# Second half of the first row tile's tokens moved from SyncE's DMA queue to ScalarE's, behind that engine's first operation

## Chip, cores and metric

The kernel runs on one core of a Trainium2 chip. The metric is device time in microseconds for one execution. Before the change the median of three runs is 414.63 us (414.38 to 415.16).

## What is computed

One block with two branches over 2048 tokens of width 448, mixed by a gate per token. Branch A is an attention with 16 heads of 28, in which each token looks at 8 keys, its own and those 2, 4, ... 14 tokens back; branch B is a two-layer network of width 1792 with a squared ReLU.

```
x = A_x                                        # (1, 2048, 448)
g = sigmoid((x * gate_w).sum(-1, keepdims=True))
q, k, v = split(x @ wqkv)                      # 16 heads of 28
a = softmax(q . k[pos - 0, 2, ..., 14] * 28**-0.5) @ v, then @ wo
b = relu(x @ w1 + b1)**2 @ w2 + b2
out = g * a + (1 - g) * b
```

The host hands x over transposed (`xT`), as four row tiles of 512 tokens; each tile has the 448 features as three full groups of 128 partitions and a fourth group of 64 that is stored twice, one copy in each half of the partitions. `wqkv`, `w1` and `wo` are laid out in the same four groups.

## The kernel before, in words

Every matrix product is made of three TensorE products: both operands are split into a rounded part ("high") and a remainder ("low"), and high times high, high times low and low times high are added up in PSUM. A split of an operand is a copy to the rounded type on ScalarE (for one half tile a copy on VectorE) and a subtraction on VectorE.

The kernel has an order written out by hand: the instructions of each engine stand in the order in which the program names them, and a small list of due times decides where loads, splits and attention pieces are put between matmuls. TensorE first makes q, k and v for the four row tiles, writes them to DRAM by way of ScalarE and SyncE's queue, and then makes the two layers of branch B and the output projection, while GpSimd and VectorE work through the attention from copies in SBUF.

All loads and stores of the kernel before are issued by SyncE (SP), one after the other, in program order. The loop at L633 to L640 issues the first ones: for each feature group `k` the q weights (`raws[0]`, called `wqraw` in the profile, L635 and L638), then the first row tile's features (`rx`, called `xraw`, L640). For group 0 the row tile comes in two transfers, tokens 0 to 255 and tokens 256 to 511, for the other groups in one. Ten transfers come out of this loop: weights 0, first token half 0, second token half 0, weights 1, tokens 1, weights 2, tokens 2, two halves of weights 3, tokens 3. Behind them SP issues the k and v weights (L645, L648). Completion counts are kept in eight semaphores that the transfers take in turn; a transfer that is the next user of a semaphore waits at the queue until the one before it has landed.

The splits of the first tile stand at L650 to L663: for each group the weights' high part on ScalarE (L651), the two token halves' high parts (ScalarE L658; group 0's first half on VectorE, L656), then the low parts on VectorE (L659 weights, L661 tokens). TensorE's first products are those of `qkv_first`: group 0 of the q products for 128-token blocks 0 and 1 (six matmuls), then for blocks 2 and 3 (six matmuls, which read the second token half), then groups 1 and 2 in the same way (all L258), then group 3 and the k and v products (L187). Ahead of them TensorE runs 13 matmuls on zeros (L628). `none` is a single element that VectorE sets to zero at L626.

Of the kernel before, what the change touches and what calls it, by code (L numbers as in the profile page):

```python
# [9 lines left out]
AF = mybir.ActivationFunctionType  # L10
# [12 lines left out]
CH = 512  # L23
# [33 lines left out]
def gated_mix_kernel(ctx: ExitStack, tc: tile.TileContext, xT, wqkv, w1, w2, wo, b1, b2, out):  # L57
    nc = tc.nc
# [42 lines left out]
    b1t, none = b1z[:, :NF], b1z[0:1, 15:16]  # L101
# [393 lines left out]
    def raw_tile(name):  # L495
        return rawp.tile([P, 4, 512], F32, tag="raw", name=name)
# [135 lines left out]
    rx = raw_tile("xraw0")  # L632
    for k in range(4):  # L633
        if k < 3:
            nc.sync.dma_start(raws[0][:, k, :NQ], wqkv[0, :, k])  # L635
        else:
            for b, rows in ((0, slice(0, 64)), (1, slice(64, P))):
                nc.sync.dma_start(raws[0][rows, k, :NQ], wqkv[b, rows, k])  # L638
        for cols in ((slice(0, 256), slice(256, CH)) if k == 0 else (slice(0, CH),)):
            nc.sync.dma_start(rx[:, k, cols], xT[0, :, k, cols])  # L640

    for b, tag in ((1, "k"), (2, "v")):
        raw = attp.tile([P, 3, D], F32, tag=tag, name=f"wqraw{b}")
# [525 lines left out]
```

## Time and profile before

| | |
|---|---|
| median of three runs | 414.63 us |
| the profiled execution | 414.51 us |
| its span, first to last instruction | 412.7 us |
| TensorE busy | 408.2 us, 99% |
| GpSimd, VectorE, ScalarE busy | 268.5, 255.7, 211.3 us |
| mean granted TensorE clock | 1.000 |

Times in the views count from the first instruction. A row of the timeline gives the start, the duration, the engine, the line and the operation with output and input, a count where neighbours were merged, and in brackets how long the engine stood idle before it and what released it. PEld is the weight load of TensorE, SPq the queue of SyncE in which DMA instructions are issued. The duration of an SPq row is that of the issue, not of the transfer; when a transfer has landed is seen from the instruction that waited for it.

### The profile page before, as it was taken

To read this page: it belongs to the slowest core of one execution; us is meant where nothing else is said; L and a number is where in the kernel's file an instruction comes from. 1 tells how busy PE (TensorE), PEld (TensorE's weight loads), DVE (VectorE), ACT (ScalarE), POOL (GpSimd) and SP (SyncE) were. 2 spreads that over 40 slices of the span, in tenths; PEclk is the share of its full clock that TensorE was granted. 3 is DMA by queue.
4 is the path that set the end of the run, shared out by engine and by line. 5 is a ranking of instruction groups with operands and counts; after the bars stand their busy time and mean duration, and the time that the engine had idled before them with its cause. 6 is when DMAs were issued, how large, how long until landed. Compare 5 with 4: busy or idle time off the path is not lost.

```text
span 412.7 us, 9327 instructions
## 1 busy us (share of the span) xinstructions
PE 408.2 (99%) x3835; PEld 378.0 (92%) x3835; DVE 255.7 (62%) x404; ACT 211.3 (51%) x477; POOL 268.5 (65%) x167
## 2 busy tenths in 40 slices
PE   8999999999999999999999999999999999999997
PEld 7999999999999999888888888989898888888996
DVE  4520433276767766777656798879576677891354
ACT  4641656388765565444565535444653254346540
POOL 0000001955999999989989899999899977940000
DMA  7989999969362315555112649764146630168304
GB/s 226 380 324 326 268 393 299 335 213 311 101 235 104 128 42 218 209 184 152 29 58 95 228 160 270 197 146 149 27 163 186 229 129 2 45 177 132 96 0 180
DMA packets 65611, 73.76 MB, mean 179 GB/s; under 512 B 32352, under 2 KB 58528, under 8 KB 65184
## 3 DMA queue, kind: packets, MB, share of 16 engines
q1 hardware_dynamic: 65568, 73.16, 55.1%
q8 instruction: 30, 0.49, 0.5%
q14 instruction: 13, 0.11, 0.1%
HBM read 45.71 MB, written 28.25 MB: 179 GB/s over the span
## 4 chain that ended last, share of the span: by engine, by line
PE 97%; DMA 1%; SPq 0%; DVE 0%; ACT 0%; issue 0%
PE b L187 33%; PE h L187 32%; PE qkv L187 23%; PE a L187 7%; PE qkv L258 1%; DMA xraw<-xT 1%; PE a L943 1%; PE last L943 0%; SPq L640 0%; SPq L635 0%; DVE bt L822 0%; ACT x L658 0%; PE last L935 0%; PE a L935 0%
## 5 line engine op out<-in xcount | busy, mean ns | idle before, releaser
L334 POOL TENSOR_TENSOR qk<-q,k 128x896 f32<-128x896 f32 x64 | 135.1, 2137 | 84.8 <-DMA k<-k_d 76.4
L341 POOL TENSOR_TENSOR av<-lg,v 128x896 f32<-128x896 f32 x64 | 119.4, 1961 | 6.3 <-DVE lg L335 5.8
L187 PE MATMUL qkv<-wqh,x 64*128 64x448 f32 (+1 forms) x528 | 89.1, 361 | 0.0
L615 DVE TENSOR_TENSOR h<-h,h 128x512 fp32r<-128x512 f32 x56 | 38.4, 688 | 65.9 <-ACT h L618 65.5
L187 PEld LDWEIGHTS qkv<-wqh,x 64*128 64x128 f32 x528 | 72.2, 184 | 0.8
L187 PE MATMUL qkv<-wql,x 64*128 64x448 f32 (+1 forms) x264 | 72.2, 360 | 0.0
L187 PE MATMUL b<-w2ah,h 64*128 64x448 f32 x448 | 68.5, 359 | 0.0
L187 PE MATMUL b<-w2bh,h 64*128 64x448 f32 x448 | 67.8, 360 | 0.0
L335 DVE TENSOR_REDUCE lg<-qk 128x32 f32<-128x896 f32 x64 | 67.0, 1074 | 0.0
L349 DVE TENSOR_REDUCE o<-av 128x112 f32<-128x896 f32 x64 | 66.4, 1070 | 0.1
L616 ACT ACTIVATE h<-h,b1z 128x512 f32<-128x512 f32 x56 | 36.7, 655 | 43.6 <-PE h L187 43.6
L187 PEld LDWEIGHTS b<-w2ah,h 64*128 64x128 f32 x448 | 46.9, 184 | 2.8
L187 PEld LDWEIGHTS b<-w2bh,h 64*128 64x128 f32 x448 | 45.3, 184 | 3.2 <-ACT h L567 0.3
L187 PEld LDWEIGHTS qkv<-wql,x 64*128 64x128 f32 x264 | 44.5, 184 | 0.4
L187 PE MATMUL b<-w2al,h 64*128 64x448 f32 x224 | 44.3, 358 | 0.0
L187 PE MATMUL b<-w2bl,h 64*128 64x448 f32 x224 | 43.2, 358 | 0.0
L206 ACT ACTIVATE st<-qkv 128x448 f32<-128x448 f32 x48 | 24.3, 546 | 34.8 <-PE qkv L187 26.9
L617 ACT ACTIVATE h<-h 128x512 fp32r<-128x512 f32 x56 | 33.5, 598 | 1.7
L618 ACT ACTIVATE h<-h 128x512 f32<-128x512 f32 x56 | 33.3, 594 | 0.0
L187 PE MATMUL h<-x,w1h 64*128 64x512 f32 x168 | 32.8, 386 | 0.0
L567 ACT ACTIVATE h<-h 128x4 fp32r<-128x4 f32 (+1 forms) x35 | 7.2, 207 | 43.1 <-PE b L187 43.0
L187 PE MATMUL h<-x2b,w1h 64*128 64x512 f32 x168 | 28.2, 386 | 0.0
(145 smaller groups left out, 728.7 us busy)
## 6 DMA issues: line engine op xcount, KB each, us to landing
k<-k_d SPq DMA_DIRECT2D x8, 840.0 KB, 6.4
v<-v_d SPq DMA_DIRECT2D x8, 840.0 KB, 4.8
x_d<-x SPq DMA_DIRECT2D x11, 512.0 KB, 6.6
q_d<-st SPq DMA_DIRECT2D x8, 448.0 KB, 4.1
k_d<-st SPq DMA_DIRECT2D x8, 448.0 KB, 4.6
v_d<-st SPq DMA_DIRECT2D x8, 448.0 KB, 5.9
w1raw<-w SPq DMA_DIRECT2D x4, 896.0 KB, 9.2
q<-q_d SPq DMA_DIRECT2D x8, 448.0 KB, 3.6
```

The costliest lines, as they stand in the source:

```text
L187: nc.tensor.matmul(acc.pt[:, :acc.n], a[rows], w[rows], start=acc.todo == acc.all, stop=acc.todo == 1)
L206: nc.scalar.activation(st[:, :, t % 2], pt[:, :D].rearrange("p (g c) -> p g c", g=G), AF.Copy)
L258: nc.tensor.matmul(acc.pt[:, :NQ], a, w, start=k == j == 0, stop=False)
L334: nc.gpsimd.tensor_mul(pr, q[:, s:s + 1].to_broadcast([P, W, C]), k[:, s:s + W])
L335: pending.append(lambda: nc.vector.tensor_reduce(lg[:, s], pr.rearrange("p w (h d) -> p w h d", h=HG), axis=AX.X, op=ALU.add))
L341: nc.gpsimd.tensor_mul(pr.rearrange("p (h d) w -> p w h d", h=HG), lg[:, s][:, :, :, None].to_broadcast([P, W, HG, DH]), v[:, s:s + W].rea ...
L349: nc.vector.tensor_reduce(o[:, g * C:(g + 1) * C], pr, axis=AX.X, op=ALU.add)
L567: nc.scalar.activation(ap, f32(ap), AF.Copy)
L615: nc.vector.tensor_sub(hl, pt, f32(hh))
L616: ops += [lambda pt=pt, r=r: nc.scalar.activation(pt, pt, AF.Relu, bias=b1t[:, f + r:f + r + 1]), lambda pt=pt, hh=hh: nc.scalar.activatio ...
L617: lambda pt=pt, hh=hh: nc.scalar.activation(hh, pt, AF.Square),
L618: lambda pt=pt, r=r, low=low: (nc.scalar.activation(pt, pt, AF.Square), at(delays[r], low))]
```

## The change

The second half of the tokens of group 0 is no longer issued by SP between the first half and the weights of group 1. ScalarE issues it, on its own queue. Just before it, a new copy of one element (`none`) into the first element of the region that the transfer will write is put at the head of ScalarE's stream; since the transfer overwrites that element, it waits for the copy. Bytes, destination and readers of the transfer stay as they were. On ScalarE the load of the function table now stands ahead of the new copy instead of ahead of the first weight copy, then come the new copy, the issue of the transfer, and the splits as before. On SP the nine other transfers of the loop follow in the same order, with nothing in the place of the moved one. The order of TensorE, VectorE and GpSimd is unchanged. As the semaphores are taken in turn, the k and v weight loads of L645 behind the loop wait for other transfers than before: the first for weights 1 (before: second token half 0), the second for tokens 1 (before: weights 1), the third for second token half 0 (before: tokens 1).

```
-        for cols in ((slice(0, 256), slice(256, CH)) if k == 0 else (slice(0, CH),)):
-            nc.sync.dma_start(rx[:, k, cols], xT[0, :, k, cols])
+        if k == 0:
+            nc.sync.dma_start(rx[:, k, :256], xT[0, :, k, :256])
+
+            nc.scalar.activation(rx[0:1, k, 256:257], none, AF.Copy)
+            nc.scalar.dma_start(rx[:, k, 256:], xT[0, :, k, 256:])
+        else:
+            nc.sync.dma_start(rx[:, k], xT[0, :, k])
```

## Prediction

> **What bounds the kernel now.** I read the page first, then what TensorE waits for, then the chain of waits over the first 16 us, then the timeline there, and last the DMA engines' share by microsecond.
>
> ```profile
> span 412.7 us, 9327 instructions
> PE 408.2 (99%) x3835; PEld 378.0 (92%) x3835; DVE 255.7 (62%) x404; ACT 211.3 (51%) x477; POOL 268.5 (65%) x167
> PE 97%; DMA 1%; SPq 0%; DVE 0%; ACT 0%; issue 0%
> ...
> PE warm L628 <- DVE b1z L626: 1.2, 1, 1.2
> PE qkv L258 <- ACT x L658: 0.3, 1, 0.3
> ...
> 7.69:409.68 401.99, 401.99 (x3810) 372.72 (x3810) 252.60 (x396) 208.00 (x472) 267.70 (x154) 1.00 0.56 179
> ...
> 2.13 0.43 SPq L635
> 2.56 0.04 issue
> 2.60 4.59 DMA xraw<-xT
> 7.20 0.02 issue
> 7.22 0.42 ACT x L658
> 7.64 0.04 issue
> 7.69 5.09 PE qkv L258 x24
> 12.78 3.28 PE qkv L187 x27
> ```
>
> TensorE has only two waits in the whole run: 1.2 us ahead of its matmuls on zeros, and 0.3 us ahead of the matmul at 7.69. From 7.69 to its last matmul, which ends at 409.68, it is busy for 401.99 of 401.99 us. So the time is the moment of that matmul plus a fixed rest: 414.51 - 7.69 = 406.82 us. The matmul at 7.69 is the first of feature group 1, and the chain says what it waits for: tokens 1, issued at 2.60 as SP's fifth transfer, land at 7.20, ScalarE copies their first half until 7.64. Whatever the change does, it does it by moving this moment, or by making a new wait behind it.
>
> ```profile
> 0.74 1.28 ACT L651 ACT_TABLE_LOAD   x1 [0.74 <-PEq L1161]
> 0.75 0.39 SPq L635 DMA_DIRECT2D wqraw<-wqkv  x1
> 1.20 0.89 SPq L640 DMA_DIRECT2D xraw<-xT  x2
> ...
> 3.45 0.58 ACT L651 ACTIVATE wqh<-wqraw 128x450 fp32r<-128x450 f32 x1 [1.42 <-DMA wqraw<-wqkv]
> 4.17 1.09 PE L258 MATMUL qkv<-wqh,x 128*128 128x450 f32 x2
> 5.27 0.58 SPq L640 DMA_DIRECT2D xraw<-xT  x1
> 5.42 0.42 ACT L658 ACTIVATE x<-xraw 128x256 fp32r<-128x256 f32 x1 [1.39 <-DMA xraw<-xT]
> 5.89 0.30 PEld L258 LDWEIGHTS qkv<-wqh,x 128*128 128x128 f32 x2 [0.17 <-ACT x L658]
> 6.05 0.58 ACT L651 ACTIVATE wqh<-wqraw 128x450 fp32r<-128x450 f32 x1 [0.21 <-DMA wqraw<-wqkv]
> 6.41 0.56 PE L258 MATMUL qkv<-wql,x 128*128 128x450 f32 x2
> 6.81 0.56 PE L258 MATMUL qkv<-wqh,x 128*128 128x450 f32 x2
> 9.22 0.72 ACT L658 ACTIVATE x<-xraw 128x256 fp32r<-128x256 f32 x2 [0.76 <-DMA xraw<-xT]
> 9.82 0.96 PE L258 MATMUL qkv<-wqh,x 128*128 128x450 f32 x4
> ```
>
> The moved transfer is the second of the pair at 1.20; its reader is ScalarE's copy at 5.42, and the six matmuls that need it begin with the weight load at 5.89. They come in pairs 0.40 apart (6.41, 6.81), so the six are through and the slot for group 1 is free at 7.21. Two numbers follow. First, group 1 cannot start before 7.21 without the moved half landing earlier, so there are 7.69 - 7.21 = 0.48 us to be won. Second, from the half's landing to the free slot it is 7.21 - 5.42 = 1.79 us, so the half may land as late as 7.69 - 1.79 = 5.90 and cost nothing.
>
> **The change part by part.**
>
> ```profile
> 1.08 0.06 DVE L626 MEMSET b1z<- 1x1 f32 x1
> ...
> L195 ACT ACTIVATE qkv<-b1z x2: 163/163/163, 13.7 to 14.3; 1x1 f32<-1x1 f32 x2
> ...
> 2.00:3.00 1.00, 1.00 (x6) 1.00 (x6) 0.00 (x0) 0.02 (x1) 0.00 (x0) 1.00 0.86 282
> 3.00:4.00 1.00, 1.00 (x7) 1.00 (x5) 0.27 (x1) 0.55 (x1) 0.00 (x0) 1.00 0.49 108
> 4.00:5.00 1.00, 1.00 (x4) 0.80 (x4) 0.96 (x3) 0.03 (x1) 0.00 (x0) 1.00 0.96 276
> 5.00:6.00 1.00, 1.00 (x6) 0.78 (x6) 0.15 (x2) 0.42 (x1) 0.00 (x0) 1.00 1.01 327
> 6.00:7.00 1.00, 1.00 (x6) 0.94 (x6) 0.63 (x2) 0.58 (x1) 0.00 (x0) 1.00 1.08 296
> ...
> xraw<-xT SPq DMA_DIRECT2D x1, 128.0 KB, 2.5
> ...
> xraw<-xT SPq DMA_DIRECT2D x1, 128.0 KB, 3.7
> ...
> xraw<-xT SPq DMA_DIRECT2D x3, 256.0 KB, 5.5
> ```
>
> The rows of 2 to 7 us end in clock, DMA share and GB/s; the last three are issues with the time from issue to landing: the first token half, the second (the one that moves), and the three 256 KB ones.
>
> The new copy. It needs `none`, set at 1.14, and the table, loaded at 2.02; a copy of one element took 163 ns, so it is over at 2.18. Nothing waits for it but the issue behind it, and ScalarE was idle until 3.45: no cost.
>
> The issue on ScalarE. At about 2.2, against 1.66 before (the pair ends at 2.09, one issue is 0.43). The trace has no DMA issued by ScalarE, so I bound it by SP's: 0.43 us each, ending at 2.63. Behind it stands the weight copy at 3.45, with 0.8 us to spare; it could take 1.2 us before anything moved, and another 0.48 us before the end moved.
>
> The moved half's landing. 2.2 + 2.5 = 4.7 by the first half's row, 2.2 + 3.7 = 5.9 by its own. The far end meets the 5.90 of above exactly; within these rows it costs nothing. The 5.5 us of the larger transfers is the outer bound: 7.7, which would put group 1 at 7.7 + 1.79 = 9.49, 1.80 us late. I take the middle of the two small rows, 5.3, since size and reader's place are theirs.
>
> SP's queue. With one issue fewer, weights 1, tokens 1 and all behind them are issued 0.47 us earlier (2.60 against 2.13 is the spacing). What that is worth at the landing lies between two ends. The engines are full from 4 to 7 (0.96 to 1.08), and by 7.20 they have to move the same bytes whichever queue they are in: then tokens 1 still land at 7.20, gain 0. But from 3 to 4 us they stood at 0.49 with weights 1 and tokens 1 already issued (2.13, 2.60), while the moved half, ahead of them in the same queue, took 3.7 us where its twin took 2.5. If that half goes beside the queue instead of in it, the 0.51 us of idle share can be used: gain up to the 0.47 by which the issue is earlier. I take 0.30, nearer to the upper end, because the row of 3 to 4 shows idle engines and issued work at once.
>
> The Trainium skill, in "DMA: Bandwidth & Descriptors", section "Issuing engines are not separate DMA queues", says that transfers from SyncE and ScalarE run on the same 16 engines and that a second issuer saves only issue time. By that rule alone this term is 0; the full engines of 4 to 7 us agree with it, the row of 3 to 4 leaves room.
>
> The waits of the L645 loads. The first now waits for weights 1 (landed by 6.05) instead of the half (5.42), and the second for tokens 1 (7.20 or earlier). The engines are full through that time with what was issued before, so I cost this at nothing; without that cover, the k weights would come up to 0.8 us later.
>
> What is late next: ScalarE has the first half of tokens 2 rounded 9.22 + 0.36 = 9.58, and group 2 starts with the third matmul of the row at 9.82, 10.22. Moved up by the full 0.48 it would start at 9.74, still behind 9.58. So the gain is kept.
>
> Sum against the profiled execution: 414.51 + 0 (copy) + 0 (issue) + 0 (half) - 0.30 (tokens 1) = 414.21 us. The median of the runs stands 0.12 above the profiled execution, so I forecast 414.3. About 0.2%, 0.83 us, is what a measurement of this kernel can tell from no change, and the gain cannot reach that by its own mechanism.
>
> **The rivals.**
>
> Nothing changes at the end. Tokens 1 are bound by the engines and land at 7.20, the half at 5.9 or before. For it: the shares of 4 to 7 us. Against it: the row of 3 to 4. Time 414.5.
>
> The half lands late (the other side). On its own queue, started 0.55 us later, it shares the 16 engines with a backlog that SP has already issued. It decides from a landing at 5.90; by 0.83 us from 6.73, which is 4.5 us after the issue. Price: landing + 1.79 - 7.69, so 0 at 5.9, +1.8 and 416.3 at 7.7. For it: transfers issued from 2.6 to 5.3 took 5.5 us. Against it: they were long because they were last in one queue.
> "DMA: Bandwidth & Descriptors" of the Trainium skill, section "Queues, rings and completion order", says that an engine takes the queues with work in turn, packet by packet; that would give the half its turn at once and speaks against this rival. No row here has two queues at work together.
>
> ScalarE is held at the issue. SP issues back to back with gaps of 0.04 us. If ScalarE's issue gets its turn only when SP stops, which after the change is at 5.85 - 0.47 = 5.38, then ScalarE's weight copy starts at 5.81 instead of 3.45 and the half lands at 7.9 to 9.1: group 1 at 9.7 to 10.9, and 416.5 to 417.7. It decides once ScalarE is held beyond 3.45 + 0.48 = 3.93. Held for one SP issue, 0.43 us, it costs at most 0.43.
> "Perfetto Trace Analysis", section "DMA Instruction — HWDGE (DVE, Sync)", in the Trainium skill says that the descriptor generator is locked for one issuer at a time and that the wait for it counts in the issue. A ScalarE issue far over 0.43 us would be that.
>
> **How the numbers follow.** Forecast 0.33 (413.9 to 414.6 with the spread of runs; 0.04 of it reads as faster). No change at the end 0.23. The half late 0.27, of which 0.06 stays within 0.83 us and 0.21 does not, since a second queue beside a full one is not seen in this trace. ScalarE held 0.09. Something I have not seen 0.08, 0.05 of it faster and 0.03 slower. So faster 0.09, same 0.29 + 0.23 + 0.06 = 0.58, slower 0.21 + 0.09 + 0.03 = 0.33. The range 413.8 to 416.3 leaves out faster below it (0.09) and the held ScalarE and the like above (about 0.1). The likeliest case's own range is 413.9 to 414.6.
>
> **What the profile after would show.** ScalarE: table load, copy of one element at about 2.0, an issue of about 0.43 us at 2.2, weight copy still at 3.45. SP: tokens 1 issued at 2.13. DMA share from 3 to 4 us above 0.49. ScalarE's copy of the moved half before 5.9, of tokens 1 at about 6.9, TensorE's group 1 at about 7.4, and no wait behind it. I am wrong if the issue on ScalarE takes over a microsecond, if the half's copy starts after 5.9, or if TensorE shows a wait after group 1 has begun.

## The result, and the profile after

The changed kernel takes 415.68 us, the median of 18 runs (415.17 to 419.96), against 414.65 us for the kernel before in 18 runs beside it (414.11 to 415.16). The medians differ by 1.03 us. The ratio of the runs lies near that of their means, so that a few long runs weigh in it: it is 1.0038, with a 95% interval of 1.0022 to 1.0053, which is 1.6 us. The kernel is slower, where 414.3 was forecast. The profiled execution took 415.78 us, its span is 413.9.

The page, what TensorE waits for, the chain of waits and the rows of the timeline that answer to those of before:

```profile
span 413.9 us, 9327 instructions
PE 408.6 (99%) x3835; PEld 378.6 (91%) x3835; DVE 257.3 (62%) x404; ACT 211.2 (51%) x478; POOL 268.6 (65%) x167
q10 hardware_dynamic: 144, 0.13, 0.1%
...
PE qkv L258 <- ACT x L663: 1.1, 1, 1.1
...
2.04 0.21 ACT xraw L642
2.25 0.02 issue
2.27 5.04 DMA xraw<-xT
7.31 0.02 issue
7.33 0.42 ACT x L663
7.76 0.04 issue
7.80 6.27 PE qkv L258 x30
...
2.13 0.43 SPq L645 DMA_DIRECT2D xraw<-xT  x1
2.27 0.37 ACTq L643 DMA_DIRECT2D xraw<-xT  x1
3.32 0.58 ACT L656 ACTIVATE wqh<-wqraw 128x450 fp32r<-128x450 f32 x1 [1.08 <-DMA wqraw<-wqkv]
4.13 1.03 PE L258 MATMUL qkv<-wqh,x 128*128 128x450 f32 x2
5.71 0.95 PE L258 MATMUL qkv<-wqh,x 128*128 128x450 f32 x2
7.80 0.67 PE L258 MATMUL qkv<-wqh,x 128*128 128x450 f32 x2 [1.14 <-ACT x L663]
8.13 0.71 ACT L663 ACTIVATE x<-xraw 128x256 fp32r<-128x256 f32 x2
8.71 0.96 PE L258 MATMUL qkv<-wqh,x 128*128 128x450 f32 x4
```

The moved half goes through a queue of its own now (q10, 144 packets, 0.13 MB). It is issued when it should be, at 2.27, and the issue takes 0.37 us; but it lands at 7.31, 5.04 us later, where it took 3.7 us before. TensorE stands idle for 1.14 us in front of the six matmuls that need it, and the chain of waits now runs through this transfer instead of tokens 1. Six matmuls behind 7.80, at 9.11 (the third of the row at 8.71), group 1 begins; before, it began at 7.69. From there to the end of the span it is 404.84 us, before 405.04. So the whole loss of this execution lies in its first nine microseconds.

The engines' share of those microseconds (last columns: clock, DMA share, GB/s):

```profile
2.00:3.00 1.00, 1.00 (x6) 1.00 (x6) 0.00 (x0) 0.23 (x2) 0.00 (x0) 1.00 0.90 300
3.00:4.00 1.00, 1.00 (x7) 1.00 (x5) 0.37 (x2) 0.58 (x1) 0.00 (x0) 1.00 0.67 129
4.00:5.00 1.00, 1.00 (x5) 0.88 (x5) 0.89 (x2) 0.00 (x0) 0.00 (x0) 1.00 0.82 257
5.00:6.00 1.00, 1.00 (x4) 0.92 (x3) 0.00 (x0) 0.00 (x0) 0.00 (x0) 1.00 1.07 274
6.00:7.00 1.00, 0.66 (x2) 0.04 (x1) 0.00 (x0) 0.00 (x0) 0.00 (x0) 1.00 0.81 239
```

The thin microsecond from 3 to 4 is still there, 129 GB/s against 108 at a share of 0.67 against 0.49, although the half is no longer in front of weights 1; and from 4 to 7 the engines move 770 KB where they moved 899 before (the sums of the GB/s column). Tokens 1, issued 0.47 us earlier, land at 7.89 instead of 7.20.

### The profile page after: what moved, and what is told of

Its sections match the earlier page's. It is cut to its first block, busy times and chain, and to the rows that moved or that the text cites. A ratio compares the mean times of both kernels' runs of the same rounds, so it can differ in the third digit from the quotient of the medians.

```text
span 413.9 us, 9327 instructions
## 1 busy us (share of the span) xinstructions
PE 408.6 (99%) x3835; PEld 378.6 (91%) x3835; DVE 257.3 (62%) x404; ACT 211.2 (51%) x478; POOL 268.6 (65%) x167
## 4 chain that ended last, share of the span: by engine, by line
PE 97%; DMA 1%; ACT 0%; DVE 0%; issue 0%
PE b L187 33%; PE h L187 32%; PE qkv L187 23%; PE a L187 7%; PE qkv L258 2%; DMA xraw<-xT 1%; PE a L948 1%; ACT L642 0%; PE last L948 0%; DVE bt L827 0%; ACT x L663 0%; PE last L940 0%; PE a L940 0%; ACT xraw L642 0%
## 5 line engine op out<-in xcount | busy, mean ns | idle before, releaser
L187 PEld LDWEIGHTS b<-w2ah,h 64*128 64x128 f32 x448 | 47.8, 184 | 2.8
L187 PE MATMUL h<-x0b,w1h 64*128 64x512 f32 x168 | 28.1, 386 | 0.0
```

The lines of the kernel that those rows point to most:

```text
L187: nc.tensor.matmul(acc.pt[:, :acc.n], a[rows], w[rows], start=acc.todo == acc.all, stop=acc.todo == 1)
```

## The experiments

The landings in this part are the last of a transfer's completion counts in the trace. "Group 1" is the start of TensorE's thirteenth product.

| kernel | half: issued, landed | tokens 1: issued, landed | group 1 | ratio to before, 95% interval |
|---|---|---|---|---|
| before | SP 1.66, 5.40 | 2.60, 7.20 | 7.69 | |
| changed | ScalarE 2.27, 7.31 | 2.13, 7.89 | 9.11 | 1.0038 (1.0022 to 1.0053) |
| changed, 2nd trace | ScalarE 2.27, 6.37 | 2.13, 8.16 | 8.65 | 1.005 (1.0023 to 1.0078) |
| changed, 3rd trace | ScalarE 2.27, 6.49 | 2.13, 7.42 | 8.29 | 1.0031 (1.002 to 1.0042) |
| copy alone | SP 1.66, 5.38 | 2.61, 6.64 | 7.19 | 1.0 (0.9992 to 1.0009) |
| SP, half behind weights 1 | SP 2.13, 6.04 | 2.60, 6.74 | 7.86 | 1.0007 (0.9998 to 1.0016) |
| ScalarE, no copy ahead | ScalarE 0.74, 4.38 | 2.13, 7.22 | 10.27 | 1.0051 (1.0038 to 1.0065) |
| half not read | ScalarE 2.27, 6.89 | 2.13, 8.08 | 8.57 | 1.0017 (1.0009 to 1.0026) |
| half left out | none | 2.13, 7.34 | 7.83 | 0.9998 (0.998 to 1.0016) |
| SP held | ScalarE 2.27, 5.14 | 3.29, 7.47 | 7.96 | 0.9999 (0.9982 to 1.0016) |
| tokens 3 on ScalarE | SP 1.66, 6.72 | 2.61, 8.45 | 9.63 | 1.0034 (1.0021 to 1.0048) |
| 7 KB on ScalarE | SP 1.65, 5.50 | 2.60, 7.21 | 7.70 | 1.0004 (0.9996 to 1.0013) |
| tokens 1 in two, all on SP | SP 1.65, 5.54 | 2.60, 6.65 and 3.08, 6.99 | 7.94 | 0.9993 (0.9977 to 1.0009) |
| changed, 22 matmuls on zeros | ScalarE 2.27, 6.51 | 2.13, 8.01 | 8.51 | 1.0036 (1.0024 to 1.0048) |

By medians the changed kernel is 1.03, 2.06 and 0.96 us above the kernel before in its three sets of runs, the half not read 0.94, the half on SP behind weights 1 0.39, SP held 0.29, the half left out 0.26. The kernel before that stood beside SP held, the half left out, tokens 1 in two and the second set of the changed kernel had four runs of 416.4 to 416.96 among 35, which pulls these ratios down.

Two theories stood at the start. T: the half is late because it is issued 0.6 us later and so gets behind weights 1. Q: a transfer on a second queue is served badly while the first queue has a backlog.

**Queue or order.** The half stays on ScalarE but goes out first; or it stays on SP but goes out behind weights 1.

```
-            nc.scalar.activation(rx[0:1, k, 256:257], none, AF.Copy)
             nc.scalar.dma_start(rx[:, k, 256:], xT[0, :, k, 256:])
```

> The transfer of the second half stays on ScalarE's queue, but the copy of one element ahead of it is gone, so it is issued at about 0.75 us, beside SP's first issue, and the table load comes behind it. Theory Q (a second queue is served badly beside a queue with a backlog, whenever its transfer is issued): the half still lands after 5.9 us and group 1 still starts after 7.69; time 414.9 to 415.7. Theory T (the half is late because it is issued 0.6 us later and so comes to the engines behind weights 1): issued first, it lands before 4.5 us; weights 0 and the first half land up to 0.4 us later; no wait for the half is left, time 414.2 to 414.7.

```
-        for cols in ((slice(0, 256), slice(256, CH)) if k == 0 else (slice(0, CH),)):
-            nc.sync.dma_start(rx[:, k, cols], xT[0, :, k, cols])
+        if k == 1:
+            nc.sync.dma_start(rx[:, 0, 256:], xT[0, :, 0, 256:])
+        cols = slice(0, 256) if k == 0 else slice(0, CH)
+        nc.sync.dma_start(rx[:, k, cols], xT[0, :, k, cols])
```

> All on SP as before the change, only the order of two transfers is exchanged: weights 1 third, the second half fourth. The half is issued at 2.13 us, close to the 2.27 of ScalarE's issue. Theory T (order and time of the issue): the half lands at 6.0 us (that is where the fourth transfer landed before), group 1 starts at 7.8, tokens 1 still land at 7.2; 414.5 to 414.8. If the half is as late as on ScalarE's queue (7.3 us), the order alone explains the change and the time is 415.4 to 415.8. Theory Q: as before or 0.1 us above, 414.5 to 414.8, with the half in by 6.1.

On SP behind weights 1 the half is issued within 0.14 us of ScalarE's issue, and lands at 6.04, as the fourth transfer should; the time is the same as before within its interval. So the later place accounts for 0.64 us of the later landing (5.40 to 6.04) but not for the loss, and T falls as its cause. But Q in the form I gave it did not hold for the first kernel: with the half issued at 0.74 it did land early, at 4.38, and the time was still 0.5% above that of before, no better than the changed kernel; its median of 416.91 is above what either theory gave. The rows show where it went:

```profile
0.74 0.41 ACTq L642 DMA_DIRECT2D xraw<-xT  x1
0.75 0.39 SPq L635 DMA_DIRECT2D wqraw<-wqkv  x1
4.21 0.58 ACT L655 ACTIVATE wqh<-wqraw 128x450 fp32r<-128x450 f32 x1 [1.75 <-DMA wqraw<-wqkv]
5.19 0.29 DVE L660 CAST x<-xraw 128x256 fp32r<-128x256 f32 x1 [4.05 <-DMA xraw<-xT]
5.63 1.09 PE L258 MATMUL qkv<-wqh,x 128*128 128x450 f32 x2 [1.29 <-DVE x L660]
```

Weights 0 come 0.76 us later than before (4.21 against 3.45), the first half 1.46 us later (5.19 against 3.73), and TensorE waits 1.29 us at the very start. Both queues pay: what is on the second queue is served at the cost of the first. Of the 2.58 us by which group 1 begins later, 1.46 are there at the first product; the rest came with the slow pace of the matmuls that is told of below.

**Half or stream.** The changed kernel, but the splits of the second half read the first half's columns (the run leaves the use of those tokens out); then the same without the transfer.

```
+    def src(k, cols):
+        return slice(0, 256) if k == 0 else cols
...
-                nc.scalar.activation(x.h[k][:, cols], rx[:, k, cols], AF.Copy)
+                nc.scalar.activation(x.h[k][:, cols], rx[:, k, src(k, cols)], AF.Copy)
...
-            nc.vector.tensor_sub(x.l[k][:, cols], rx[:, k, cols], f32(x.h[k][:, cols]))
+            nc.vector.tensor_sub(x.l[k][:, cols], rx[:, k, src(k, cols)], f32(x.h[k][:, cols]))
```

> The changed kernel, but the splits of the second half of group 0 read the first half's columns, so nothing but SP's semaphore waits for the moved transfer (the output for those tokens is then that of other tokens in this group). If the late half is the whole cost: group 1 starts no later than before, 414.1 to 414.7. If the second queue also slows the other transfers (tokens 1 landed at 7.89 in the changed kernel against 7.20): group 1 starts at about 8.4, time 415.0 to 415.3.

```
-            nc.scalar.activation(rx[0:1, k, 256:257], none, AF.Copy)
-            nc.scalar.dma_start(rx[:, k, 256:], xT[0, :, k, 256:])
```

> The run in which nobody reads the moved half, now also without its transfer and without the copy ahead of it (the tokens of the second half of group 0 are not loaded; the first half's are used for them). If it is the transfer on the second queue that slows SP's transfers: tokens 1 land at 6.7 or earlier, against 8.08 with it, and the time goes down to 414.0 to 414.6. If something else delays them (the missing place of the half in SP's order, for one): tokens 1 stay near 8.0 and the time near 415.2.

The chain of waits with the half transferred and not read:

```profile
2.13 5.95 DMA xraw<-xT
8.08 0.02 issue
8.10 0.42 ACT x L667
8.53 0.04 issue
8.57 5.09 PE qkv L258 x24
```

Nobody waits for the half, and the kernel is still 0.17% slower: tokens 1 take 5.95 us from issue to landing, where they took 4.59 before. Without the transfer the time is that of the kernel before within its interval, and tokens 1 land at 7.34, between the 6.7 and the 8.0 of the two expectations. So the transfer on ScalarE's queue costs twice: once by landing late itself, once by slowing SP's transfers. By medians the second alone came to nearly the whole loss, 0.94 us; but the intervals of these two kernels overlap, and the landings are of one trace each. How much of the loss is the one or the other can't be added up, since TensorE waits for whichever ends last: for the half in the first and third traces of the changed kernel, for tokens 1 in the second. The run without the transfer says one thing more. It has 128 KB less to move ahead of tokens 1 and issues them 0.47 us earlier than the kernel before, and they don't land earlier (7.34, against 7.20 and 6.64 in two kernels with the half in SP's order). Taking the half out of SP's order gained nothing that these runs can tell.

**The backlog taken away.** One more copy of one element behind ScalarE's issue, into the place of weights 1, keeps SP from issuing weights 1 until 2.92.

```
             nc.scalar.dma_start(rx[:, k, 256:], xT[0, :, k, 256:])
+            nc.scalar.activation(raws[0][0:1, 1, 0:1], none, AF.Copy)
```

> The changed kernel with one more copy of one element on ScalarE, behind the issue of the half, into the place where weights 1 will be written. SP cannot issue weights 1 until that copy is over, at about 2.9 us, and all of SP's later transfers come 1.2 us later; so the half meets an empty backlog. Theory Q (the half is late because it shares the engines with SP's backlog): it lands at 4.8 to 5.4 us, and group 1 is bound by tokens 1 alone, which land between 7.2 and 8.4; 414.5 to 415.7. If ScalarE's queue is slow by itself: the half still lands after 6.5.

```profile
2.27 0.38 ACTq L643 DMA_DIRECT2D xraw<-xT  x1
2.92 0.33 SPq L635 DMA_DIRECT2D wqraw<-wqkv  x1
3.29 0.43 SPq L646 DMA_DIRECT2D xraw<-xT  x1
5.17 0.42 ACT L664 ACTIVATE x<-xraw 128x256 fp32r<-128x256 f32 x1 [1.11 <-DMA xraw<-xT]
7.49 0.72 ACT L664 ACTIVATE x<-xraw 128x256 fp32r<-128x256 f32 x2 [0.98 <-DMA xraw<-xT]
...
xraw<-xT ACTq DMA_DIRECT2D x1, 128.0 KB, 2.9
```

The last row is the half's issue with its time to landing. The same issue on the same queue at the same moment lands after 2.9 us instead of 5.04, 4.10 and 4.22 in the three traces of the changed kernel. ScalarE's queue is not slow by itself. And tokens 1, issued 1.16 us later than in the changed kernel, land no later there (7.47, against 7.42 to 8.16). The time is that of the kernel before within its interval; by medians 0.29 us are left, and group 1 begins 0.27 us later than before. Issuing SP's transfers later undid most of the loss.

**Other transfers on the second queue.** The half goes back to SP. Instead tokens 3 (256 KB, needed last) go out by ScalarE; or nothing but an early extra load of the bias vector, 7 KB in as many rows as the half has.

```
+        if k == 3:
+            nc.scalar.activation(rx[0:1, k, 0:1], none, AF.Copy)
...
-            nc.sync.dma_start(rx[:, k, cols], xT[0, :, k, cols])
+            (nc.scalar if k == 3 else nc.sync).dma_start(rx[:, k, cols], xT[0, :, k, cols])
```

> The half is back in its place on SP; instead tokens 3 (256 KB, not read before 10.5 us) are issued by ScalarE behind the copy of one element, at 2.27 us. Theory Q in its strong form (any transfer on a second queue early on slows SP's transfers): the half lands after 5.6, tokens 1 after 7.5, and group 1 starts at 8.0 or later; 414.9 to 415.6. If only the transfer on the second queue suffers: the half and tokens 1 as before (5.4, 6.6 to 7.2), 414.3 to 414.8.

```
+    nc.scalar.activation(b1t[0:1, 0:1], none, AF.Copy)
+    nc.scalar.dma_start(b1t, b1)
     raws = [raw_tile("wqraw0")]
```

> The kernel before, with all its transfers on SP, and beside them one small transfer on ScalarE's queue behind a copy of one element: the bias vector b1, 7 KB in 128 rows of 56 bytes, which is loaded here already and again later. It has as many rows as the moved half and a twentieth of its bytes. If it is turns (packets) on the second queue that delay SP's transfers: tokens 1 after 7.4, 414.8 to 415.4. If it is bytes, or the queue does no harm as such: 414.3 to 414.7, tokens 1 at 6.6 to 7.2.

With tokens 3 on ScalarE the half, in its old place on SP, lands at 6.72 and tokens 1 at 8.45: the strong form of Q, SP's transfers are slowed by what they share the engines with. (The median of 416.49 is above the 415.6 expected; the slow pace told of below is part of it.) The 7 KB do no harm to SP's transfers (7.21 for tokens 1), which points to bytes as what hurts them. But they need as long themselves: the last of their completion counts comes at 6.51, 4.24 us after the issue, as long as for 128 KB. So it is not its own bytes that make a transfer on the second queue late. The DMA view by half microseconds counts the packets of ScalarE's queue, 144 each time. In the changed kernel 2 of them are moved from 3.5 to 4.0 us, then 7, 39, 70, 20, 3 and 3 up to 7.0. For the 7 KB it is 1 from 3.0 to 3.5, then 10, 48, 64, 13 and 8 up to 6.0; with SP held, 14 from 3.0 to 3.5, then 77, 48 and 5 up to 5.0. So most packets are moved behind 4.5 us beside the backlog, large or small, and before 4.5 without it; and in the changed kernel the last six, behind 6.0, make the landing of 7.31. What they wait for is not shown.

**The copy alone.** The one element goes to a place that nothing reads, and all transfers stay on SP.

```
+    nc.scalar.activation(b1z[0:1, 14:15], none, AF.Copy)
     raws = [raw_tile("wqraw0")]
```

> The kernel before with the copy of one element at the head of ScalarE's stream, writing an element that nothing reads, and all transfers on SP. Both theories: no cost, 414.5 to 414.8, with the table load and the copy over by 2.3 us and the weight copy where it was.

Ratio 1.0: the copy and the table load ahead of it cost nothing, as expected.

**The room ahead of group 1.** The kernel before with tokens 1 in two transfers.

```
-        for cols in ((slice(0, 256), slice(256, CH)) if k == 0 else (slice(0, CH),)):
+        for cols in ((slice(0, 256), slice(256, CH)) if k < 2 else (slice(0, CH),)):
```

> The kernel before, all on SP, with tokens 1 also sent as two halves. ScalarE's copies of tokens 1 are halves already, and TensorE's first six products of group 1 need only the first. It tests the 0.48 us that the prediction found to be won ahead of group 1: the first half should land 0.5 us before the whole did, group 1 start between 7.2 and 7.69; 414.0 to 414.6, which a median of this kernel hardly tells from no change.

The first half of tokens 1 lands at 6.65, the second at 6.99. Ratio 0.9993 (0.9977 to 1.0009), no change that can be told: in its trace the matmuls of group 0 ran at the slow pace of the next paragraph, and group 1 began only at 7.94. No kernel of this study beats the one before.

**The pace of the first matmuls.** In the kernel with tokens 3 on ScalarE the matmuls stay slow long after the wait:

```profile
7.21 1.12 PE L258 MATMUL qkv<-wqh,x 128*128 128x450 f32 x2 [0.56 <-ACT x L660]
8.13 0.95 PE L258 MATMUL qkv<-wql,x 128*128 128x450 f32 x2
8.88 1.70 PE L258 MATMUL qkv<-wqh,x 128*128 128x450 f32 x4
10.38 0.78 PE L258 MATMUL qkv<-wql,x 128*128 128x450 f32 x2
...
9.00:10.00 1.00, 1.00 (x4) 0.87 (x3) 0.69 (x2) 0.74 (x2) 0.00 (x0) 1.00 1.07 302
```

Two matmuls take 0.75 us from start to start (8.13 to 8.88, then four in 1.50), where it is 0.40 in the kernel before from 6.41 on, and the granted clock reads 1.00 all the same. It ends at 11 us. The kernel with the half issued first shows the same until 10.3; both had TensorE idle (0.56 and 1.29 us) within the first eight microseconds. The changed kernel's own three traces, with 1.14, 1.08 and 0.82 us idle, were at the fast pace behind the wait, so idle time does not always do it. So I tried to take the idle time away with more matmuls on zeros, beside another run of the changed kernel.

```
-WARM = 13
+WARM = 22
```

> The changed kernel with 22 instead of 13 matmuls on zeros, which keep TensorE busy until about 6.2 us, so that its first products come later but the wait for the half hardly leaves it idle. Theory P (some of the loss, and all of the runs above 416.5, come from TensorE's matmuls staying at 0.375 us apart instead of 0.20 for another stretch when it stands idle in the first microseconds): no run above 416.5, spacing 0.20 from the half on, median 415.0 to 415.8. If the pace has no part in it and the half and tokens 1 alone set the time: median and tail as in the changed kernel, runs up to 417 and more.

> The changed kernel once more, beside the run with 22 matmuls on zeros: median 415.5 to 416.7, and if theory P holds one run in four above 416.5.

The second trace of the changed kernel came with an earlier run, under this expectation:

> The changed kernel once more, for a second trace: theory Q expects the half to land again after 6.3 us, tokens 1 later than the 7.2 of before, and no wait of TensorE behind group 1; 415.2 to 416.5.

With 22 the median is 415.87 (415.10 to 416.61, 6 runs), with 13 beside it 415.51 (415.12 to 417.76, 11 runs): no gain, and one of its six runs is above 416.5 against one of eleven, so the expectation on the tail is not met. In its trace the zeros end at 5.77 and not at 6.2 as expected, but TensorE shows no wait any more, the matmuls run at the fast pace from the first product on, and group 1 still begins only at 8.51, behind tokens 1, which land at 8.01. So the loss does not need the slow pace. As to the long runs, what speaks for the pace is only this: of the 37 runs of the changed kernel 7 have a mean granted clock of 0.996 or less, and all 7 took 417.1 us or more; none of the six with 22 matmuls and none of the runs of the kernel before that stood beside the experiments is below 0.998. Against it: the granted clock read 1.00 all through the slow pace, so that 0.996 may be something else; one run of the changed kernel took 418.51 at 1.000; and the four long runs of the kernel before, 416.4 to 416.96, are at 1.000 too. Four of the seven are among the eight runs of the second set, whose median of 416.72 is above the 416.5 expected. No such run was caught in a profile. What makes the long runs stays open.

## Why the prediction was wrong, point by point

**What bounds the kernel: right.** The rest behind group 1 is fixed. Span less the start of group 1 is 405.04 before, 404.84, 404.96 and 404.88 in three traces of the changed kernel, 405.04 with the half not read, 405.06 with SP held. Only the kernels with tokens 3 (405.47) and with 7 KB (405.26) on ScalarE have a few tenths more, the former by the slow matmuls.

**Copy and issue on ScalarE: right.** 0.20 us and 0.37 us, at 2.04 and 2.27; the weight copy at 3.32 waited for neither. ScalarE was not held at the issue: it overlaps SP's at 2.13, and SP's spacing stayed 0.47, so that rival is out. The Trainium skill's lock on the descriptor generator ("Perfetto Trace Analysis", section "DMA Instruction — HWDGE (DVE, Sync)") shows in no row here: two issues at 0.74 and 0.75 took 0.41 and 0.39 us side by side.

**The moved half's landing: the step that failed.** I set it to 5.3, between two rows of its size, and it was 7.31 (6.37 and 6.49 in the other traces), each time past the 5.90 up to which it would have cost nothing. The rows of the same size were transfers at the front of one queue; the row that resembled it was that of the 256 KB transfers, 5.5 us, which had a backlog beside them as well. I had it as the outer bound and took size for the likeness. Size was the wrong likeness: 7 KB took 4.24 us on that queue. The nearest row in time was among the lines shown: weights 1, issued at 2.13, released ScalarE's copy at 6.05. By that row the half lands at about 6.1, which is already too late, and on SP in that place it did land at 6.04. The second queue added 0.3 to 1.3 us to that.

**The 0.30 us from SP's queue: failed with the wrong sign.** The idle share from 3 to 4 us was not due to the half in front of weights 1. With the half elsewhere the share is 0.67, as I had said, but at 129 GB/s little more is moved, and with the half left out altogether tokens 1 still land at 7.34. And I had the second queue as a help to SP's transfers; with it they landed 0.2 to 1.0 us later than in the kernel before, in spite of an issue 0.47 us earlier.

**The rivals.** "The half lands late" is what happened. Its working was right: landing 7.31 + 1.79 = 9.10, and group 1 began at 9.11, which is 1.42 us late in the trace; 6.49 + 1.79 = 8.28 in the third trace, and it began at 8.29. In the second it is 8.16, and tokens 1 held group 1 until 8.65: that the second queue would delay SP's transfers was in none of the rivals. The measured 415.68 lies inside the stated range only because the range took in this rival; the forecast had the sign wrong. I gave this rival 0.27 because I knew no row with two queues and let the rule of turns ("DMA: Bandwidth & Descriptors" of the Trainium skill, section "Queues, rings and completion order") speak against it. The turns are no guarantee of an early landing: the sixteen parts of the half finish between 5.47 and 7.31, before between 4.09 and 5.40, and the last one counts. The rule in the section "Issuing engines are not separate DMA queues" of the same page of the Trainium skill, that a second issuer saves only issue time, is right as to the gain; that it can cost was shown only by the runs.

**What hid behind.** No wait followed behind group 1, as said; ScalarE's copies of tokens 1 (8.13) came ahead of their slot in this trace, but in the second one TensorE waited for them once more, 0.3 us.

## What to carry to other kernels

In this kernel a transfer that is needed soon did not belong on a second queue next to a queue that had several transfers waiting: it landed 0.3 to 1.3 us later than in the same place of the one queue (6.37 to 7.31 against 6.04), and the backlog paid too. Look for the price in rows with the same neighbours, not the same size. Where the order of the first loads matters, one queue with the order written out keeps it; here, beside a second queue, issuing SP's next loads 1.2 us later was worth more than issuing them early.

## What I had not expected

The 7 KB that took 4.24 us on the second queue. The thin microsecond from 3 to 4, 97 to 147 GB/s in the traces of the kernel before, the changed one, the copy alone, tokens 3 on ScalarE and SP held, whichever transfer is third. Only the kernel that issues the half first moves 253 GB/s there, and then 185 in the microsecond behind it. The cause is open. And tokens 1 landing at 7.20 in one trace and 6.64 in another (the copy alone, whose profiled run of 413.98 was the shortest of its eleven) with the same transfers on SP in the same order: a step of half a microsecond in the start of this kernel is within what one trace differs from the next.
